# S4 convolution and gated feed-forward on one core: the first table's inputs go to the head of one queue, the spectrum products are merged, and the order ahead of the gate tiles is rewritten

## The chip, the cores and the metric

The kernel runs on one core of a Trainium2 chip. The metric is the device time of one execution in microseconds (us). Three runs of the kernel before took 786.79, 787.2 and 788.53 us; the median is 787.2. The profile comes from a further execution that took 788.84 us, of which the trace shows a span of 787.0 us from the first to the last instruction.

## The reference

The block takes a sequence of 2048 tokens of 448 channels through a state-space convolution and a gated feed-forward network, both conditioned by one vector `c`.

```python
mod = (_silu(c) @ w_mod).reshape(c.shape[0], 6, 1, -1)     # sa, ca, ga, sb, cb, gb
h = _layernorm(x) * (1 + ca) + sa
x = x + ga * S4(h)
h = _layernorm(x) * (1 + cb) + sb
x = x + gb * ((_gelu(h @ w_gate) * (h @ w_up)) @ w_down)
# S4(h): dt = exp(log_dt);  P = exp(dt * A * l) for l = 0..2047   (complex)
#        K = real(sum over n of C * P * (dt * B));  y = irfft(rfft(h) * rfft(K)) + h * Dskip
```

There are 448 channels with 256 complex states each. The kernel `K` (448 x 2048) has to be generated from the parameters before it can be transformed.

## The kernel before, in words

Every piece of work is a task with a name, made by `add(name, {engine: ...}, ...)`. The table `PLACE` gives each task a number. `Plan.run` sorts all tasks by that number and lets each issue its instructions in that order, so the table alone decides what follows what on each engine's in-order queue. A letter behind a number chooses the engine where a task may run on several (`a` ScalarE, `d` VectorE, `s` SyncE's queue, `p` GpSimd's). In the trace ScalarE is ACT, VectorE DVE, TensorE PE, GpSimd POOL and SyncE SP.

The program has four stages.

1. **Preparation.** `prep(t)` turns the parameters of 112 channels into two tables of logarithms and phases (`p.A1` to `p.f1`), split into bf16 pieces, written to memory (`p.put0`, `p.put1`, tile `lh_d`) and read back in another layout (`lt0`, `lt1`, tile `lt`). It needs the six parameter planes `in_abc` (`p.ld`: four planes, then two) and the step `dt` (`c.ld`, `dt`). For the first table its steps on ACT are `p.S1` (squares, absolute values), `p.S2` (logarithm, line 569), `p.S3` (exponential, line 570), `p.S4` (arctangent, line 580). Functions of different kinds need ACT_TABLE_LOAD ahead of them. At the same time the modulation rows come from `w_mod` (`m.ld`, `m.mm`, `m.ev`), and the input is normalised (`bn`, `norm`).
2. **Table stage (the K stage below).** For each of 56 sub-blocks of 8 channels: PE multiplies the small tables (`x.mm`, `y.mm`, `ang`), ACT takes exponentials (tiles `mx` and `my`), sines and cosines (`fg`), DVE forms the products `tx` (line 721) and `ty` (line 725), and PE sums over the states (`kgen`, line 748; tile `kg`). Every two sub-blocks are evacuated (`kev`, tile `ke`), turned (`ka`) and stored (`kout`, tile `ako`). `NMY` is the number of `my` buffers. Beside that runs the transform of the input (`ub`, `ub.ev`, tile `uo`) and, from about 205 us, the transform of `K` for two groups of channels, in 11 batches each (`k_fft`): `f.fwd` (line 1094), the spectrum product `f.pr` (line 1098), `f.inv` (line 1105), `f.z` (tile `zo`), `f.st`.
3. **Transition.** The third group is transformed with all engines free (`t_fft`). Its results go through memory: `t.s0` stores to `yb_d` (line 1224), `yi.l0` and `yi.l1` read it back (line 1297, tile `yi`). Then the residual (`co.mml`, line 1409; `co.addl`), the second layer norm, and the first gate tile. The first weights `w` are loaded meanwhile (`w.le`, line 1332). `spin` tasks are matrix products whose result is not used.
4. **Gate tiles.** Gate and up products (`gu`, lines 1524 and 1530) and down products (line 1630), for four blocks of 512 tokens.

A DMA is given one of eight completion semaphores in turn, and an issue waits until the earlier transfer on its semaphore has landed; `waits DMAHW4` in the listings below is such a wait (or one for data). The queue of SP issues in order, so a transfer that waits holds all behind it.

Of the kernel before, what the change touches and what calls it, by code (L numbers as in the profile page):

```python
# [15 lines left out]
AF = mybir.ActivationFunctionType  # L16
# [24 lines left out]
    "anc": "125 131 142 164 160 200 209 244 266 311 327 339 347 355 438 456 470 487 499 524",  # L41
    "ang": "114 115 130 146 158 162 204 212 241 298 319 324 341 350 421 443 454 476 496 506 511 591 602 610 654 670 690 698 "
        "741 761 764 775 792 795 805 885 894 905 908 927 932 950 1007 1018 1021 1034 1039 1051 1115 1124 1135 1151 1157 "
        "1169 1187 1197",
    "as": "66d 64d 79d 107d 116d 151d 119d 185a 250d 258d 265a 289d 309d 333d 334d 365d",
    "bn": "47 50 54 49 9 20 10 17 227 243 235 239 187 224 197 210",
    "c.ai": "1257",
    "c.ak": "177",
    "c.au": "62",
    "c.c": "21",  # L50
    "c.ea": "59",
    "c.ih": "1283",
    "c.ld": "11",
    "c.rd": "58",
    "c.t1": "219",
    "co.adde": "1329 1347 1366 1355",
    "co.addl": "1384 1387 1421 1410",
    "co.addx": "1495 1510 1499 1522 1672 1712 1735 1684 1791 1803 1809 1801",
    "co.ca": "1404a 1408a 1456a 1441a",
    "co.cb": "1415d 1416a 1459a 1448a",  # L60
    "co.h0": "1398a 1403a 1447d 1430a",
    "co.h2": "1534a 1580a 1571a 1562a 1748a 1744d 1755a 1760d 1848d 1882a 1833a 1866a",
    "co.l0": "1402 1405 1449 1434",
    "co.l2": "1541 1585 1573 1577 1749 1751 1757 1761 1849 1885 1843 1876",
# [36 lines left out]
    "dn3h": "1997 1999",
    "dn4": "1746 1889 1987",
# [1731 lines left out]
```

## Time and profile before

| what | value |
|---|---|
| median of three runs | 787.2 us |
| profiled execution: its time, its span | 788.84 us, 787.0 us |
| PE busy | 728.1 us, 93% of the span |
| DVE busy | 591.6 us, 75% |
| ACT busy | 459.5 us, 58% |
| POOL busy | 9.0 us, 1% |
| mean granted TensorE clock | 0.991 |
| moved by DMA | 139.87 MB |

Shares over the whole span hide that the stages differ. Before 336 us, ACT and DVE are nearly always busy; after 393 us only PE is. The first table product on PE starts at 28.39 us, the first exponential on ACT at 29.74 us, the first gate tile at 392.57 us. The profile's parts are: busy time of the engines, the span in slices, DMA queues, the chain of work that ended last, the costliest groups of instructions, and DMA issues. The trace also answers with a timeline (start, duration, engine, line, operation, and in brackets what ended the idle time ahead of it) and with busy times in chosen stretches.

### The profile page before, as it was taken

Reading aid. Unit: us, or ns where it says so; the run is one execution under the profiler, and the core shown is the slowest. Engines: PE = TensorE matmul, PEld = TensorE weight load, DVE = VectorE, ACT = ScalarE, POOL = GpSimd, SP = SyncE. Lnnn points to the kernel's source line nnn. Section 1 sums busy time; section 2 is a strip of 40 time slices with the busy share of each in tenths; the row PEclk is TensorE's granted clock in tenths of the full one; section 3 lists DMA queues with packets and bytes.
Section 4 is the critical chain, followed back from the end, with each engine's and each line's share of the span. In section 5 each row is a group of like instructions: output and inputs, shape, how many; then the busy total and the mean of one; then the engine's idle time right before and its main releaser. Section 6 shows DMA issues by size and latency. Waiting matters only on the chain.

```text
span 787.0 us, 19037 instructions
## 1 busy us (share of the span) xinstructions
PE 728.1 (93%) x8166; PEld 443.6 (56%) x8166; DVE 591.6 (75%) x893; ACT 459.5 (58%) x611; POOL 9.0 (1%) x24
## 2 busy tenths in 40 slices
PE   1786889998899999989999999999999999999998
PEld 0333454543667767768784445444595446944478
DVE  5989999999999999988768851469773587133743
ACT  4799999899999999961555640233421244012320
POOL 0000000000000000000300000000000000000000
PEclk9989899999999999999999999999999999999999
DMA  9654458997878767999697875345447324012201
GB/s 260 180 162 141 142 148 242 298 263 225 255 232 223 222 190 212 290 294 252 193 311 231 273 191 159 129 129 188 164 67 206 111 94 134 14 47 94 82 2 59
DMA packets 103790, 139.87 MB, mean 178 GB/s; under 512 B 34388, under 2 KB 85268, under 8 KB 103706
## 3 DMA queue, kind: packets, MB, share of 16 engines
q1 hardware_dynamic: 99940, 131.61, 57.0%
q10 hardware_dynamic: 3206, 6.07, 2.3%
q8 instruction: 64, 1.05, 0.6%
q0 software_dynamic: 560, 0.98, 0.4%
q14 instruction: 20, 0.16, 0.1%
HBM read 100.39 MB, written 36.01 MB: 173 GB/s over the span
## 4 chain that ended last, share of the span: by engine, by line
PE 69%; DVE 4%; ACT 4%; DMA 2%; issue 2%; SPq 1%; DVEq 0%; ACTq 0%
PE pq L1530 31%; PE pq L1630 9%; PE pf L1105 4%; PE pd L1599 4%; PE kg L748 4%; PE pf L1094 3%; PE pg L675 2%; PE pq L1524 2%; PE kg L771 2%; PE pd L1630 2%; DVE ty L725 1%; PE pd L1404 1%; PE pg L657 1%; ACT fg L692 1%; PE pf L1189 1%
## 5 line engine op out<-in xcount | busy, mean ns | idle before, releaser
L1530 PE MATMUL pq<-ht,wr 128*128 128x512 f16 (+1 forms) x1200 | 248.5, 365 | 1.3 <-DMA ht<-hl 1.2
L1530 PEld LDWEIGHTS <-wr 128*128 128x128 f16 x1200 | 114.5, 98 | 130.0 <-issue 13.0
L725 DVE TENSOR_TENSOR ty<-my,fg 128x2048 f32<-128x2048 f32 x56 | 127.5, 2283 | 0.8 <-issue 0.5
L1537 ACT ACTIVATE ge<-pq 128x512 f32<-128x512 f32 (+1 forms) x60 | 33.9, 565 | 102.1 <-PE pq L1524 68.7
L1544 DVE TENSOR_TENSOR fq<-ge,pq 128x512 f32<-128x512 f32 (+1 forms) x60 | 38.9, 649 | 71.5 <-PE pq L1530 44.3
L1556 ACT ACTIVATE hh<-fq 128x1024 f16<-128x1024 f32 (+1 forms) x49 | 46.7, 961 | 64.9 <-DVE fq L1544 46.4
L721 DVE TENSOR_TENSOR tx<-mx,fg 128x1024 f32<-128x1024 f32 x56 | 67.7, 1218 | 2.4 <-ACT fg L692 1.0
L1630 PE MATMUL pq<-d,hh 128*128 128x224 f16 x476 | 68.9, 259 | 0.0
L748 PE MATMUL kg<-ty,tx 128*32 128x64 f32 x3584 | 63.6, 222 | 4.7 <-issue 2.6
L748 PEld LDWEIGHTS kg<-ty,tx 128*32 128x32 f32 x3584 | 53.8, 111 | 23.8 <-issue 15.7
L1559 DVE TENSOR_TENSOR hlo<-fq,hh 128x1024 f16<-128x1024 f32 (+1 forms) x49 | 53.7, 1106 | 12.9 <-ACT hh L1556 12.7
L1630 PE MATMUL pq<-d,hlo 128*128 128x224 f16 x238 | 61.6, 259 | 0.0
L688 ACT ACTIVATE fg<-pg 128x1024 f32<-128x1024 f32 x56 | 58.0, 1038 | 1.2 <-PE pg L675 0.8
L662 ACT ACTIVATE my<-pg 128x1024 f32<-128x1024 f32 x56 | 55.5, 1031 | 2.0 <-PE pg L657 1.9
L1630 PEld LDWEIGHTS <-hh 128*128 128x128 f16 x560 | 54.1, 98 | 0.9 <-issue 0.2
L1105 PE MATMUL pf<-q,fc 128*128 128x160 f32 x264 | 41.5, 307 | 1.1 <-DVE q L1098 1.1
L692 ACT ACTIVATE fg<-fg,small 128x1024 f32<-128x1024 f32 x36 | 41.5, 1170 | 0.1
L1747 ACT ACTIVATE d<-fq 128x896 f16<-128x896 f32 x14 | 13.3, 947 | 46.1 <-PE pd L1599 27.3
L1105 PEld LDWEIGHTS pf<-q,fc 128*128 128x128 f32 x264 | 36.4, 190 | 6.5 <-issue 1.5
L675 PEld LDWEIGHTS <-lt 64*128 64x128 bf16 x304 | 18.0, 96 | 38.8 <-issue 26.5
L675 PE MATMUL pg<-ea,lt 64*128 64x512 bf16 x152 | 30.5, 392 | 7.6 <-ACT fg L699 3.4
L984 PE MATMUL pf<-ui,fu 128*128 128x448 f32 x66 | 31.0, 575 | 1.6 <-ACT uo L480 1.4
(210 smaller groups left out, 1117.6 us busy)
## 6 DMA issues: line engine op xcount, KB each, us to landing
wr<-w_d SPq DMA_DIRECT2D x21, 896.0 KB, 5.2
fc<-in_k_fc SPq DMA_DIRECT2D x20, 576.0 KB, 3.7
u_d<-so SPq DMA_DIRECT2D x32, 224.0 KB, 2.8
ui<-u_d SPq DMA_DIRECT2D x10, 672.0 KB
fq<-in_wd SPq DMA_DIRECT2D x14, 448.0 KB, 6.1
w<-in_wgu SPq DMA_DIRECT2D x11, 512.0 KB, 7.4
us<-uo SPq DMA_DIRECT2D x22, 240.0 KB, 5.2
q<-us SPq DMA_DIRECT2D x22, 240.0 KB, 6.4
```

Source lines behind the costliest of these rows:

```text
L662: A.activation(yb.tile.rearrange("p h (n k) -> p n h k", n=2), pb.tile.rearrange("p (n h k) -> p n h k", n=2, h=2), AF.Exp)
L675: T.matmul(pa[:, nh * 512:nh * 512 + 512], w, x, start=(k == 0), stop=(k == 2))
L688: A.activation(fb.tile[:, 0].rearrange("p x (n k) -> p n x k", n=2), pb.tile.rearrange("p (n x k) -> p n x k", n=2, x=2), AF.Sin, scale=TW ...
L692: A.activation(fb.tile[:, 1], fb.tile[:, 1], AF.Sin, scale=-TWO_PI, bias=halfpi)
L721: V.tensor_mul(tx.tile, xb.tile[:, xm, None, :].to_broadcast([128, 2, 512]), fb.tile[:, :, 0])
L725: V.tensor_mul(ty.tile, yb.tile[:, :, None, :].to_broadcast([128, 2, 2, 512]), fb.tile[:, None, :, 1].to_broadcast([128, 2, 2, 512]))
L748: T.matmul(kg[32 * g:32 * g + 32, 2 * (s % 2) + q, :64], tx[:, r, nh, 4 * q + g], ty[:, 0:4:3, nh, 4 * q + g] if r else ty[:, 1:3, nh, 4 * ...
L1105: T.matmul(pz.tile[:, e % 32 - sl0], fc.tile[:, i, 1 + t], pp.tile[:, t, i], start=(t == 0 and e != 32), stop=(t == 1 and e != 0))
L1530: T.matmul(pb.tile[k][:, ts], wr.tile[:, 4 * lo + t, k, c0:c0 + 128], ht[:, m, ts], start=f % 2 == 0 and i == 0, stop=f % 2 == 1 and i == 9)
L1556: A.activation(hg.tile[0][:, cb, c], fq.tile[:, c], AF.Copy)
L1559: V.tensor_sub(hg.tile[1][:, cb, c], fq.tile[:, c], hg.tile[0][:, cb, c])
L1630: T.matmul(bank(k)[:, m], x[:, p, q[0], ts], w[:, p, q[1]], start=new and m == 0 and p == 0 and z == 0, skip_group_check=True, stop=i in ( ...
```

## The change

- The first table's two parameter loads move from ACT's queue to SP's: the first is SP's first transfer, ahead of `ld`, `c` and the tokens `xt`; the second follows `xt`. The write of constant ones to `lh_d` (`pad`) moves from POOL's queue to SP's.
- In `prep`, the logarithm is kept in another slot, so that the exponential of it no longer has to precede the scaled copy. For the first table two one-element activations load the table of the logarithm (`pre.ln`) and of the arctangent (`pre.at`) ahead of their use.
- The spectrum product of a batch is one DVE instruction over 2 x 480 elements, in which the second factor is read twice, in place of two over 480 elements.
- `NMY` is 12 in place of 9. The room comes from POOL's descriptor space in SBUF, 2048 bytes per partition in place of the default.
- `PLACE` has new numbers for everything ahead of the gate tiles; behind them the numbers move by 2 and the order stays. Evacuations are dealt out anew: ACT has 19 of the 28 `ke` copies in place of 11, 15 of the 16 `uo` copies in place of 11, 17 `so` in place of 19, 9 `zo` copies of 480 columns in place of 13, 6 of the casts of `lh` in place of 8; DVE has the rest. The number of ACT_TABLE_LOADs is 43 in both kernels, the number of matrix products is the same.

```diff
 PLACE = {
-    "c.ld": "11",
+    "c.ld": "3",
...
-    NMY, NMX = 9, 5
+    NMY, NMX = 12, 5
...
+    PRE_LN = add("pre.ln", {"ACT": 0.2}, -8.4, lambda: A.activation(dump, eps, AF.Ln), [t_dt], table=LN)
...
-            (dma if t else adma)(b3.tile[:, :2] if i else b1.tile, a["abc"][t, :, 4:] if i else a["abc"][t, :, :4])
+            dma(b3.tile[:, :2] if i else b1.tile, a["abc"][t, :, 4:] if i else a["abc"][t, :, :4])
...
-        PAD[t] = add("pad", {"SP": 0.7} if t else {"POOL": 1.0}, v0 + 0.5, lambda: (dma if t else P.dma_start)(lh_d[t, :, :, 6:], a["k_one"][t]), [L0], kb=300)
+        PAD[t] = add("pad", {"SP": 0.7}, v0 + 0.5, lambda: dma(lh_d[t, :, :, 6:], a["k_one"][t]), [L0], kb=300)
...
-        S2 = op("S2", {"ACT": 0.28}, lambda: A.activation(x(10), x(3), AF.Ln), [B1, L3], LN, k=0.6)
-        S3 = op("S3", {"ACT": 0.28}, lambda: A.activation(x(2), x(10), AF.Exp, scale=0.5), [S2], EXP, k=0.65)
+        S2 = op("S2", {"ACT": 0.28}, lambda: A.activation(x(7), x(3), AF.Ln), [B1, PRE_LN if t == 0 else None], LN, k=0.6)
+        S3 = op("S3", {"ACT": 0.28}, lambda: A.activation(x(2), x(7), AF.Exp, scale=0.5), [S2], EXP, k=0.65)
...
+        pre_at = add("pre.at", {"ACT": 0.2}, v0, lambda: A.activation(dump, eps, AF.Arctan), [S3], table=ATAN) if t == 0 else None
...
-        B2 = op("B2", {"ACT": 0.28}, lambda: A.activation(x(10), x(10), AF.Identity, scale=0.5, bias=ld[:, t:t + 1]), [S2, S3], k=0.7)
+        B2 = op("B2", {"ACT": 0.28}, lambda: A.activation(x(10), x(7), AF.Identity, scale=0.5, bias=ld[:, t:t + 1]), [S2, L3], k=0.7)
...
         def prod():
-            for t in range(2):
-                V.tensor_mul(pp.tile[:, t, :ne], ut.tile[:, t, :ne], pk.tile[:, :ne])
+            V.tensor_mul(pp.tile[:, :, :ne], ut.tile[:, :, :ne], pk.tile[:, None, :ne].to_broadcast([128, 2, ne, n]))
...
-    nc = _bacc.Bacc("TRN2", target_bir_lowering=False, num_devices=1)
+    nc = _bacc.Bacc("TRN2", target_bir_lowering=False, num_devices=1, dynamic_dma_scratch_size=2048)
```

The lines of the changed program stand 2 to 5 numbers later than those of the program before (569 is 573, 1098 is 1102, 1332 is 1336).

**SP's queue at the start.** `in_abc` are the parameters, `in_A_u` the tokens, `in_w_mod` the modulation weights, `lh_d` the table written by line 595. Before:

```order
L852 DMA xt<-in_A_u 128x1792
L486 DMA ld<-in_A_log_dt 112x4
L486 DMA c_sb<-in_c 112x4
L805 DMA fg<-in_w_mod 112x1792 x3
L852 DMA xt<-in_A_u 128x1792
L595 DMA lh_d<-lh 112x1536
L486 DMA rd<-in_k_rd 128x1025
L486 DMA ea<-in_k_ea 128x1536
L486 DMA au<-in_k_au 128x128
L620 DMA lt<-lh_d 64x7x128 x2
```

Now:

```order
L515 DMA q<-in_abc 112x1024
L488 DMA ld<-in_A_log_dt 112x4
L488 DMA c_sb<-in_c 112x4
L857 DMA xt<-in_A_u 128x1792
L515 DMA q<-in_abc 112x512
L810 DMA fg<-in_w_mod 112x1792 x2
L857 DMA xt<-in_A_u 128x1792
L810 DMA fg<-in_w_mod 112x1792
L518 DMA lh_d<-in_k_one 224x512
L600 DMA lh_d<-lh 112x1536
```

The parameters and the ones stand in this queue now; `rd`, `au`, `ea` and the two `lt` loads follow as before.

**ACT in the preparation.** Line 551 is `p.S1`, 569 `p.S2`, 570 `p.S3`, 561 and 577 the copies `p.A3` and `p.B2`, 564 and 565 `p.C1`, 792 the sigmoid of `c`. Before:

```order
L564 ACTIVATE q<-q,dts__106 112x256
L565 ACTIVATE q<-q 112x256
L551 ACTIVATE q<-q 112x512
L552 ACTIVATE q<-q 112x256
L569 ACT_TABLE_LOAD
L569 ACTIVATE q<-q 112x256
L792 ACT_TABLE_LOAD
L792 ACTIVATE sig<-c_sb 112x4
L561 ACTIVATE q<-q,dts__106 112x256
L570 ACTIVATE q<-q 112x256
L577 ACTIVATE q<-q,ld 112x256
```

Now:

```order
L555 ACTIVATE q<-q 112x512
L556 ACTIVATE q<-q 112x256
L500 ACT_TABLE_LOAD
L500 ACTIVATE small<-small 128x1
L573 ACTIVATE q<-q 112x256
L568 ACTIVATE q<-q,dts__106 112x256
L569 ACTIVATE q<-q 112x256
L582 ACTIVATE q<-q,ld 112x256
L565 ACTIVATE q<-q,dts__106 112x256
L574 ACT_TABLE_LOAD
L574 ACTIVATE q<-q 112x256
L580 ACT_TABLE_LOAD
```

The load for the logarithm no longer waits for line 558 of DVE; the four copies stand between the logarithm and the exponential now.

**SP's queue at the end of the transition,** from the last store of the third group's results to the last of their read-backs. Before:

```order
L1224 DMA yb_d<-z_5275 128x128 [waits DMAHW3_49,Activation_49]
L1332 DMA w<-in_wgu 128x1024 [waits DMAHW4_49,DVE_49,PE_49]
L1297 DMA yi<-yb_d 8x2x512 [waits DMAHW7_49,DMAHW5_49]
L1297 DMA yi<-yb_d 6x2x512 [waits DMAHW6_49]
L1297 DMA yi<-yb_d 8x2x512
L1297 DMA yi<-yb_d 6x2x512 [waits DMAHW2_49]
L1297 DMA yi<-yb_d 8x2x512 [waits DMAHW3_49]
L1297 DMA yi<-yb_d 8x2x512 [waits DMAHW4_49]
```

Now:

```order
L1336 DMA w<-in_wgu 128x1024 [waits DMAHW3_49,DVE_49,PE_49]
L1301 DMA yi<-yb_d 8x2x512 [waits DMAHW4_49]
L1301 DMA yi<-yb_d 6x2x512 [waits DMAHW5_49]
L1228 DMA yb_d<-z_5248 128x128 [waits DMAHW7_49,DVE_49]
L1301 DMA yi<-yb_d 8x2x512 [waits DMAHW1_49,DMAHW0_49]
L1301 DMA yi<-yb_d 6x2x512 [waits DMAHW2_49]
L1301 DMA yi<-yb_d 8x2x512 [waits DMAHW3_49]
L1301 DMA yi<-yb_d 8x2x512 [waits DMAHW4_49]
L1301 DMA yi<-yb_d 8x2x512 [waits DMAHW7_49,DMAHW5_49]
```

The weight load stands ahead of the last store now. It is also the transfer whose semaphore a read-back near the end takes over.

More of the change, by code (lines that the diff above doesn't have):

```diff
@@ L510, in ld1 @@
                 b1.tile = pq.tile([DT, 4, N], FT, name="q")
-            (dma if t else adma)(b3.tile[:, :2] if i else b1.tile, a["abc"][t, :, 4:] if i else a["abc"][t, :, :4])
-        L0 = add("p.ld", {"SP" if t else "ACT": 0.42 if t else 0.1}, v0, lambda: ld1(0), (), [b1], (), kb=459)
-        PAD[t] = add("pad", {"SP": 0.7} if t else {"POOL": 1.0}, v0 + 0.5, lambda: (dma if t else P.dma_start)(lh_d[t, :, :, 6:], a["k_one"][t]), [L0], kb=300)
+            dma(b3.tile[:, :2] if i else b1.tile, a["abc"][t, :, 4:] if i else a["abc"][t, :, :4])
+        L0 = add("p.ld", {"SP": 0.42}, v0, lambda: ld1(0), (), [b1], (), kb=459)
+        PAD[t] = add("pad", {"SP": 0.7}, v0 + 0.5, lambda: dma(lh_d[t, :, :, 6:], a["k_one"][t]), [L0], kb=300)
         L3 = add("p.al", {"NONE": 0.0}, v0, al3, (), [b3])
-        L1 = add("p.ld", {"SP" if t else "ACT": 0.42 if t else 0.1}, v0, lambda: ld1(1), [L0, L3], (), [b3], kb=230)
+        L1 = add("p.ld", {"SP": 0.42}, v0, lambda: ld1(1), [L0, L3], (), [b3], kb=230)
         def op(n, e, fn, deps, table=None, alloc=(), use=(), k=0.0):
@@ L575, in slope @@
             V.tensor_mul(x(5), x(5), x(1))
+        pre_at = add("pre.at", {"ACT": 0.2}, v0, lambda: A.activation(dump, eps, AF.Arctan), [S3], table=ATAN) if t == 0 else None
         D1 = op("D1", {"DVE": 2.41}, slope, [S3], k=0.75)
-        B2 = op("B2", {"ACT": 0.28}, lambda: A.activation(x(10), x(10), AF.Identity, scale=0.5, bias=ld[:, t:t + 1]), [S2, S3], k=0.7)
+        B2 = op("B2", {"ACT": 0.28}, lambda: A.activation(x(10), x(7), AF.Identity, scale=0.5, bias=ld[:, t:t + 1]), [S2, L3], k=0.7)
         B3 = op("B3", {"DVE": 0.33}, lambda: V.tensor_add(x(10), x(10), x(4)), [B2], k=0.8)
         P0 = pieces(0, l0, lambda: pair(b3, 1), [A3, B3], 0.9)
-        S4 = op("S4", {"ACT": 0.28}, lambda: A.activation(x(5), x(5), AF.Arctan), [D1], ATAN, k=1.0)
+        S4 = op("S4", {"ACT": 0.28}, lambda: A.activation(x(5), x(5), AF.Arctan), [D1, pre_at], ATAN, k=1.0)
         G1 = op("G1", {"DVE": 0.33}, lambda: V.scalar_tensor_tensor(x(11), x(6), 126.0 / math.pi, x(0), op0=OP.mult, op1=OP.add), [C2, B1], k=0.9)
@@ L586, in phase @@
             V.scalar_tensor_tensor(x(7), x(11), -0.25 * math.pi, x(7), op0=OP.mult, op1=OP.add)
-        E1 = op("E1", {"DVE": 0.66}, phase, [S4, G1], k=1.1)
+        E1 = op("E1", {"DVE": 0.66}, phase, [S4, G1, B2], k=1.1)
         E2 = op("E2", {"ACT": 0.28}, lambda: A.activation(x(11), x(7), AF.Copy, bias=MAGIC), [E1], k=1.2)
```

440 rows, old and new, of the table PLACE are left out of this document.

## The prediction

> **What bounds the kernel now.** I read the busy times by stage first, because shares of the whole span mix stages with different limits. The columns are the stretch, its length, the busy time of PE, its weight loads, DVE, ACT and POOL with counts, then the TensorE clock, the DMA share and GB/s.
>
> ```profile
> 0.00:29.00 29.00, 11.70 (x31) 4.78 (x32) 18.77 (x46) 14.76 (x25) 1.51 (x11) 1.00 0.82 232
> 29.00:205.00 176.00, 147.23 (x2417) 74.41 (x2417) 167.88 (x232) 168.19 (x217) 0.00 (x0) 0.96 0.71 206
> 205.00:336.00 131.00, 128.51 (x2466) 95.77 (x2459) 126.03 (x129) 125.98 (x147) 0.00 (x0) 1.00 0.77 230
> 336.00:393.00 57.00, 51.35 (x806) 43.04 (x798) 47.70 (x79) 25.37 (x48) 6.83 (x12) 1.00 0.84 241
> 393.00:787.00 394.00, 389.31 (x2480) 225.60 (x2477) 231.24 (x411) 125.18 (x179) 0.69 (x1) 1.00 0.45 135
> ```
>
> The reader is to see four limits. Up to 29 us no engine is busy: a chain of steps and transfers sets the time. From 29 to 336 us DVE (293.9 of 307) and ACT (294.2) are both at 96%, and from 205 us PE is at 98%. From 336 to 393 us a chain runs over several engines. After 393 us PE is at 99%, and as the change leaves the order there as it was, I cost those 394 us at nothing: PE itself is the cover. A gain can come from the first 393 us only, and whatever starts the gate tiles earlier moves the end by as much.
>
> Next the timeline of the preparation (start, duration, engine, line, shapes, idle time ahead and its cause).
>
> ```profile
> 7.87 1.23 DVE L542 TENSOR_TENSOR q<-q 112x1024 f32<-112x1024 f32 x1 [6.96 <-DMA q<-in_abc]
> ...
> 12.54 1.28 ACT L569 ACT_TABLE_LOAD   x1 [0.76 <-DVE q L558]
> ...
> 13.83 0.42 ACT L569 ACTIVATE q<-q 112x256 f32<-112x256 f32 x1
> ...
> 14.27 1.28 ACT L792 ACT_TABLE_LOAD   x1
> ...
> 16.07 0.40 ACT L570 ACTIVATE q<-q 112x256 f32<-112x256 f32 x1
> ...
> 17.39 0.42 DVE L573 SCALAR_TENSOR_TENSOR q<-q 112x256 f32<-112x256 f32 x1
> ...
> 21.15 0.69 DVE L538 TENSOR_TENSOR lh<-q,lh 112x512 bf16<-112x512 f32 x1
> ...
> 21.92 0.31 SPq L595 DMA_DIRECT2D lh_d<-lh  x1
> ...
> 24.95 1.35 SPq L620 DMA_DIRECT2D lt<-lh_d  x2
> ...
> 28.40 0.28 PE L638 MATMUL pg<-rd,lt 64*128 64x256 bf16 x1 [0.69 <-DMA lt<-lh_d]
> ...
> 27.91 0.53 ACT L833 ACTIVATE gs<-pf 128x448 f32<-128x448 f32 x1
> 29.74 1.02 ACT L644 ACTIVATE mx<-pg 128x1024 f32<-128x1024 f32 x1
> ```
>
> The chain is: parameters land at 7.87, logarithm 13.83, exponential 16.07, the first pieces are split by 21.84, their store is issued at 21.92, the read-back at 24.95 (it waits for the store, 3.03), the first product at 28.40, the first exponential of the table stage at 29.74.
>
> **Part 1, the start.** The parameters shared the engines with the tokens. Now their 448 KB go first. The rows of 2 us give the rates:
>
> ```profile
> 0.00:20.00 20.00, 3.56 (x11) 1.30 (x12) 10.18 (x27) 9.75 (x16) 1.51 (x11) 1.00 0.91 258
> ...
> 0.00:2.00 2.00, 0.00 (x0) 0.00 (x0) 0.09 (x2) 0.32 (x1) 1.24 (x11) 1.00 0.36 47
> ...
> 4.00:6.00 2.00, 0.00 (x0) 0.00 (x0) 0.00 (x0) 0.00 (x0) 0.00 (x0) 1.00 1.02 317
> ...
> 12.00:14.00 2.00, 0.00 (x0) 0.00 (x0) 1.93 (x7) 1.45 (x2) 0.00 (x0) 1.00 0.99 247
> ...
> 20.00:22.00 2.00, 2.00 (x4) 0.77 (x4) 1.93 (x5) 0.42 (x1) 0.00 (x0) 1.00 0.02 7
> ```
>
> Transfers begin near 1.7 us (47 GB/s in the first 2 us); 459 kB at 247 to 317 GB/s take 1.5 to 1.9 us, so with about half a us to report the first product of the preparation starts near 4.3, 3.6 earlier. The logarithm gains another 1.0, since its load no longer stands between DVE and it: -4.6. Then four copies (0.45 each, an estimate from the 0.40 of line 570) and a load stand ahead of the exponential: 0.42 + 1.8 + 1.28 = 3.5 in place of 2.24, so -3.3. DVE has nothing else to finish when the exponential ends (before, line 573 came 0.9 after it): -4.2, and the store is issued at 17.7.
>
> There it meets what the move put ahead of it. SP's queue holds 5.16 MB before the store: by the row of the first 20 us (258 GB/s x 20 us) that is all that moved until the DMA engines fell idle (0.02 in 20 to 22 us). Nothing was taken away, so the queue is empty at about 20.0 again, and the store lands 2.7 later (as 22.23 to 24.95), at 22.7: -2.3. If all went at 317 GB/s, the queue would be empty at 18.0, and the gain would be capped by the rows of modulation: their last weights are the next thing late, with line 833 behind them, at about -3.1. If SP's queue alone goes at 247, it is empty at 22.6 and the store lands at 25.3: +0.4. **Start: -2.3, between -3.1 and +0.4**, by the row over 20 us, which holds the same transfers.
>
> The 247 GB/s stand where SP's queue was alone, the 317 where ACT's and POOL's queues ran beside it. [...]
>
> The two one-element activations cost 0.2 each and are covered: the first while DVE works on the squares, the second while it works on the reciprocal; without that cover they would cost 0.4. [...] The trace has the next activation 0.01 behind the load (12.54 + 1.28 to 13.83), and so I take 1.28.
>
> **Part 2, the table stage.** Prices are from start to start, since neighbours overlap:
>
> ```profile
> 322.14 0.57 ACT L480 ACTIVATE zo<-pf 128x480 f32<-128x480 f32 x1
> ...
> 322.59 0.39 ACT L480 ACTIVATE ke<-kg 128x252 f32<-128x252 f32 x1
> ...
> 322.85 1.04 ACT L680 ACTIVATE fg<-pg 128x1024 f32<-128x1024 f32 x1
> ...
> 333.34 0.41 DVE L482 COPY ke<-kg 128x252 f32<-128x252 f32 x1
> ...
> 333.67 0.15 DVE L766 TENSOR_TENSOR ke<-kg,d 128x4 f32<-128x4 f32 x1
> ...
> 328.80 1.21 DVE L1098 TENSOR_TENSOR q<-q,pf 128x480 f32<-128x480 f32 x2
> ...
> 329.93 0.16 DVE L766 TENSOR_TENSOR ke<-kg,d 128x4 f32<-128x4 f32 x1
> ...
> 330.00 1.22 DVE L721 TENSOR_TENSOR tx<-mx,fg 128x1024 f32<-128x1024 f32 x1
> ...
> 331.13 2.29 DVE L725 TENSOR_TENSOR ty<-my,fg 128x2048 f32<-128x2048 f32 x1
> ...
> 338.50 0.38 ACT L480 ACTIVATE ke<-kg 128x252 f32<-128x252 f32 x1 [1.34 <-PE kg L748]
> ```
>
> A pair of products occupies DVE for 1.13 us, and so does one product of 1024 elements; one of 960 is 64 elements shorter, about 0.07. The merging gives 22 x 0.07 = 1.5 us, not the 22 x 0.14 that durations without overlap suggest (two of 0.65 against 1.22 - 0.07). Eight `ke` copies less are 8 x 0.33 = 2.6 us of DVE. The other copies that change sides (`uo`, `zo`, `so`, `lh`, one `mag`), by the same rows and their widths, give back 1.5. DVE: -2.6. ACT: eight `ke` at 0.26 and four `uo` at 0.43, against four `zo` of 480 at 0.45, two `so`, two casts and one `mag` of 0.90: +0.3. ACT and DVE are equally full, so neither number is the term by itself; half of their sum is -1.15. PE has the same work. I take **-1.0**. One end is -6, if half of the 13 us that DVE and ACT each idle in this stage went with the rewritten order; the other is +3.9, if the `ke` and `uo` copies (2.1 + 1.8) all fall on ACT while it is the bound. The three further `my` buffers let exponentials run further ahead; ACT waits for no `my` buffer that I found, so I cost them at nothing.
>
> **Part 3, the transition.** The chain of work that ended last, SP's queue and PE:
>
> ```profile
> 375.52 0.32 SPq L1224 DMA_DIRECT2D yb_d<-z  x1
> ...
> 375.95 0.37 SPq L1332 DMA_DIRECT2D w<-in_wgu  x1
> ...
> 375.95 6.04 DMA w<-in_wgu
> ...
> 382.00 2.65 DMA yi<-yb_d
> ...
> 380.79 1.46 PE L1035 MATMUL pq<-idenh 128*128 128x512 f16 x6
> ...
> 385.11 0.66 PE L1409 MATMUL pd<-yi,ai 128*64 128x128 f32 x8 [1.11 <-DMA yi<-yb_d]
> ```
>
> The last read-back waited 6.04 us for a weight load that it does not use: it took over that load's semaphore. The load was held behind the last store (375.52). Now it stands ahead of it and may go about 2 us earlier. PE gets there earlier as well: it idled 1.11, and the idle products of 1.46 that stood ahead now stand behind. **-1.5**, between -2.6 (both of those) and 0, if the load waits for its buffer anyway. Next late is the layer norm between line 1409 and the first gate tile at 392.57, unchanged. The table load for the square root leaves this stretch; ACT was idle around it, so it counts nothing. POOL's transfers gain no work.
>
> **Sum.** -2.3 - 1.0 - 1.5 = -4.8. Against the profiled execution's own 788.84 (span 787.0 and 1.84 around it) that is 784.0; that execution was 1.64 above the median, so against the median 787.2 it is 782.4.
>
> **Rivals.** *More slack goes* (the end of part 2): -6 in place of -1.0 gives 777.4. For it speaks that three engines at 96 to 98% leave gaps that only an order decides; against it that the work of each is nearly unchanged. *The start gives nothing*: one queue at 247 GB/s, +0.4, and a transition at 0 with it, as its rows are about DMA too: 786.6. *ACT held by its copies*: each `ke` copy on ACT waits for PE's sums; the row at 338.50 lost 1.34 so. If the eight new ones all do, 8 x (1.34 + 0.26) = 12.8 replaces the -1.0: 796.2; it turns the change into a loss from three such waits on. Against it: most `ke` copies on ACT show no wait. *POOL starved by its smaller descriptor space*:
>
> ```profile
> yi<-yb_d POOLq DMA_DIRECT2D x9, 32.0 KB, 4.5
> ...
> 374.53 3.34 POOL L1297 DMA_DIRECT2D yi<-yb_d  x6
> ```
>
> Nine read-backs of 4.5 us, issued within 10 us now; one at a time they take 40, so +30, 812. Against it: they are small.
>
> **How the numbers follow.** Changes under 0.2% (1.6 us) cannot be told from none here. The forecast has 0.5, with its own range 779 to 785.5; more slack 0.2; nothing at the start 0.16; held copies 0.1; POOL 0.04. Faster: 0.5 + 0.2 and a little of the third, 0.73. Same: the rest of the third, 0.13. Slower: 0.14. From the ends -3.1 - 6 - 2.6 = -11.7 (775.5) and, with the third rival and a single held copy, +0.8 (788.0), the range is 776 to 788.
>
> **What would show it.** The first line-546 product near 4.3 us; the store at line 600 issued near 17.7 and the read-back near 22.7; the first exponential at 27.0 to 27.5; the last products of the table stage some 3 us earlier; a read-back that waits less than 6 us for `w`, and the first gate tile near 388. I would be wrong if the store waits longer in the queue than 5 us, if ACT shows new waits for PE ahead of `ke`, or if the gain of the first 30 us is given back before 336 because PE, and not ACT, sets the pace there.

## The result, and the profile after

The changed kernel takes 783.74 us (median of seven runs, 780.68 to 787.76); the kernel before, on the same chip, 787.2. The ratio is 0.9945, with a 95% interval of 0.9922 to 0.9967: 4.3 us less, between 2.6 and 6.1. A second set of eleven runs of the same program gave 0.9953 (0.9932 to 0.9974). The forecast was 782.4, range 776 to 788. Three single executions that took over 1.5% longer than the fastest of their kernel (one of after_again, one of tokens_fill, and one of queue_undone with 1463 us) are left out of all ratios and means.

The profiled execution took 782.35 us with a span of 780.4. Its busy times by stage, with the last cut 2 us behind the first gate tile (386.86); columns as in the prediction (PE, weight loads, DVE, ACT, POOL, granted clock, DMA share, GB/s):

```profile
0.00:29.00 29.00, 12.77 (x38) 5.09 (x39) 21.17 (x51) 18.01 (x30) 0.87 (x10) 1.00 0.83 245
29.00:205.00 176.00, 146.99 (x2440) 75.86 (x2439) 170.58 (x223) 171.06 (x227) 0.00 (x0) 0.99 0.73 209
205.00:336.00 131.00, 126.79 (x2544) 95.73 (x2546) 124.46 (x111) 124.73 (x145) 0.00 (x0) 1.00 0.84 241
336.00:389.00 53.00, 49.08 (x686) 42.11 (x683) 44.98 (x82) 23.01 (x42) 7.56 (x13) 1.00 0.79 232
389.00:780.00 391.00, 387.46 (x2464) 224.25 (x2462) 229.17 (x405) 122.77 (x175) 0.00 (x0) 1.00 0.44 134
```

Between 29 and 205 us DVE and ACT each do some 2.8 us more than before, and in the granted clock 0.99 stands where 0.96 stood. From the first gate tile to the end of the span it is 393.5 us, before 394.4. There PE waited once, for a transfer, and after the change it waits for none:

```profile
464.18 0.38 PE L1530 MATMUL pq<-ht,wr 128*128 128x512 f16 x1 [1.23 <-DMA ht<-hl]
```

The table stage alone, from the first exponential to the end of the last `kgen` product, before and after:

```profile
29.74:352.24 322.50, 288.59 (x5232) 181.07 (x5234) 308.05 (x370) 304.03 (x375) 0.00 (x0) 0.98 0.74 219
27.18:345.80 318.62, 284.55 (x5232) 180.79 (x5234) 306.15 (x343) 303.66 (x380) 0.00 (x0) 0.99 0.78 226
```

It is 3.9 us shorter. DVE's work fell by 1.9 us and its idle time by 2.0 (14.45 to 12.47), ACT's work by 0.4 and its idle time by 3.5 (18.47 to 14.96). The start, from the timeline:

```profile
4.47 1.23 DVE L546 TENSOR_TENSOR q<-q 112x1024 f32<-112x1024 f32 x1 [3.56 <-DMA q<-in_abc]
...
8.58 0.63 DVE L882 BATCH_NORM_STATS2 st<-xt 128x6 f32<-128x448 f32 x1 [2.09 <-DMA xt<-in_A_u]
...
9.80 0.42 DVE L560 TENSOR_TENSOR q<-q 112x256 f32<-112x256 f32 x1
...
10.84 0.42 ACT L573 ACTIVATE q<-q 112x256 f32<-112x256 f32 x1 [1.87 <-DVE q L562]
...
14.21 0.42 ACT L574 ACTIVATE q<-q 112x256 f32<-112x256 f32 x1
...
18.93 0.34 SPq L600 DMA_DIRECT2D lh_d<-lh  x1
...
22.00 1.35 SPq L625 DMA_DIRECT2D lt<-lh_d  x2
...
25.30 0.28 PE L643 MATMUL pg<-rd,lt 64*128 64x256 bf16 x1
...
27.18 1.02 ACT L649 ACTIVATE mx<-pg 128x1024 f32<-128x1024 f32 x1
```

The first product starts 3.4 earlier, the logarithm (10.84) 3.0, the store 3.0, the read-back 2.95, the first exponential 2.56. The parts of the chain of work that ended last in the transition:

```profile
368.48 3.74 DMA w<-in_wgu
...
375.21 3.46 DMA idenh<-in_k_ih
378.78 0.66 PE pd L1413 x8
```

The instructions around them:

```profile
370.60 0.37 SPq L1228 DMA_DIRECT2D yb_d<-z  x1
...
375.01 0.54 POOL L1301 DMA_DIRECT2D yi<-yb_d  x1 [2.50 <-DMA yb_d<-z]
...
386.86 2.35 PE L1534 MATMUL pq<-ht,wr 128*128 128x256 f16 x20
```

The chain names the constant `idenh`, which this product does not read; POOL's last read-back, issued at 375.01 after it had waited 2.50 for the last store, would land at about 378.7 by the median of these transfers (3.7). From the last store to the residual product it is now 8.18 us (370.60 to 378.78), before 9.59. The wait for `w` is 3.74 in place of 6.04.

What the column of the clock hides in long stretches shows in rows of 2 us. Before:

```profile
34.00:36.00 2.00, 1.34 (x8) 0.58 (x9) 1.89 (x5) 1.91 (x4) 0.00 (x0) 1.00 0.72 169
36.00:38.00 2.00, 0.80 (x6) 0.52 (x7) 2.00 (x6) 2.00 (x5) 0.00 (x0) 0.67 0.92 272
38.00:40.00 2.00, 2.00 (x8) 0.56 (x8) 1.28 (x5) 1.83 (x3) 0.00 (x0) 0.50 0.37 133
40.00:42.00 2.00, 2.00 (x12) 0.99 (x10) 1.51 (x5) 1.68 (x2) 0.00 (x0) 0.50 0.00 0
42.00:44.00 2.00, 2.00 (x12) 0.75 (x9) 0.41 (x2) 1.94 (x2) 0.00 (x0) 0.62 0.00 0
44.00:46.00 2.00, 1.53 (x16) 0.62 (x12) 2.00 (x4) 1.74 (x2) 0.00 (x0) 1.00 0.25 56
```

After, the only such place of the whole trace:

```profile
70.00:72.00 2.00, 0.65 (x22) 0.28 (x11) 1.90 (x7) 2.00 (x4) 0.00 (x0) 1.00 0.00 2
72.00:74.00 2.00, 1.33 (x40) 0.91 (x43) 1.97 (x4) 2.00 (x4) 0.00 (x0) 0.89 0.03 8
74.00:76.00 2.00, 2.00 (x46) 1.20 (x38) 2.00 (x4) 1.97 (x3) 0.00 (x0) 0.50 0.00 0
76.00:78.00 2.00, 2.00 (x12) 0.77 (x9) 1.77 (x6) 1.53 (x3) 0.00 (x0) 0.76 0.00 0
```

PE runs at half its clock for 6.8 us before (the missing shares 0.33 + 0.50 + 0.50 + 0.38 of 2 us are 3.4 us of clock, twice that in time), and once more so from 77.7 to 84.5; after, for 3.4 us. Each follows a stretch in which PE had little to do (0.65 of 2 us after; before, 0.52 at 74 to 76 us for the second). What the other engines do meanwhile differs. The two stretches before and the one after:

```profile
36.70:43.50 6.80, 5.95 (x24) 2.52 (x24) 4.09 (x12) 6.25 (x9) 0.00 (x0) 0.50 0.28 99
77.70:84.50 6.80, 6.21 (x80) 3.04 (x76) 6.76 (x14) 6.11 (x9) 0.00 (x0) 0.50 0.05 17
73.60:77.00 3.40, 3.40 (x66) 1.89 (x57) 3.36 (x9) 2.91 (x5) 0.00 (x0) 0.50 0.02 5
```

In the first, DVE is idle for 2.7 us, waiting for PE's products (0.41 of 2 us busy at 42 to 44 us). In the other two DVE stays busy and ACT is idle for 0.7 and 0.5 us.

### The profile page after: what moved, and what is told of

The parts are those of the page before. It is cut to its first block, busy times and chain, and to the rows that moved or that the text cites. A ratio compares the mean times of both kernels' runs of the same rounds, so it can differ in the third digit from the quotient of the medians.

```text
span 780.4 us, 18984 instructions
## 1 busy us (share of the span) xinstructions
PE 723.1 (93%) x8166; PEld 443.0 (57%) x8166; DVE 590.4 (76%) x868; ACT 459.6 (59%) x616; POOL 8.4 (1%) x23
## 4 chain that ended last, share of the span: by engine, by line
PE 69%; ACT 12%; DMA 4%; DVE 3%; issue 2%; SPq 1%; DVEq 0%; ACTq 0%
PE pq L1534 31%; PE pq L1634 9%; PE pd L1603 4%; PE kg L753 4%; PE pf L1109 4%; PE pg L680 3%; ACT my L667 2%; PE pq L1528 2%; PE pf L1099 2%; ACT fg L693 2%; PE kg L776 2%; PE pd L1634 2%; DMA us<-uo 2%; ACT fg L697 2%; PE pf L989 1%
## 5 line engine op out<-in xcount | busy, mean ns | idle before, releaser
L753 PE MATMUL kg<-ty,tx 128*32 128x64 f32 x3584 | 61.7, 222 | 2.2 <-issue 1.3
L1109 PE MATMUL pf<-q,fc 128*128 128x160 f32 x264 | 41.4, 307 | 0.3 <-issue 0.3
L697 ACT ACTIVATE fg<-fg,small 128x1024 f32<-128x1024 f32 x36 | 41.4, 1163 | 0.0
L776 PE MATMUL kg<-ak,ke 128*64 128x128 f32 x448 | 30.5, 279 | 3.4 <-DVE ke L771 3.4
```

Of the source, the lines that this page charges most:

```text
L697: A.activation(fb.tile[:, 1], fb.tile[:, 1], AF.Sin, scale=-TWO_PI, bias=halfpi)
L753: T.matmul(kg[32 * g:32 * g + 32, 2 * (s % 2) + q, :64], tx[:, r, nh, 4 * q + g], ty[:, 0:4:3, nh, 4 * q + g] if r else ty[:, 1:3, nh, 4 * ...
L1109: T.matmul(pz.tile[:, e % 32 - sl0], fc.tile[:, i, 1 + t], pp.tile[:, t, i], start=(t == 0 and e != 32), stop=(t == 1 and e != 0))
```

## The experiments

The ratio is to the runs of the kernel before on the same chip, with its 95% interval; the clock is the mean of the mean granted clocks of these runs. Behind it stands what one profiled execution of each shows, in us: first exponential, from there to the end of the last `kgen` product, clock lost to half clock between 29 and 336 us (the missing shares in rows of 2 us, added up), from the last `kgen` product to the first gate tile.

| kernel | ratio (95%) | clock | first exp. | table stage | clock lost | transition |
|---|---|---|---|---|---|---|
| before | 1 | 0.988 | 29.74 | 322.5 | 6.8 | 40.3 |
| after | 0.9945 (0.9922-0.9967) | 0.996 | 27.18 | 318.6 | 1.7 | 41.1 |
| after_again | 0.9953 (0.9932-0.9974) | 0.996 | 28.29 | 318.6 | 3.4 | 41.5 |
| start_alone | 0.9993 (0.9973-1.0013) | 0.988 | 28.28 | 322.9 | 10.3 | 42.2 |
| table_order_undone | 1.0003 (0.9974-1.0032) | 0.986 | 28.61 | 321.0 | 8.5 | 43.5 |
| trans_order_undone | 0.9960 (0.9942-0.9979) | 0.995 | 28.06 | 320.7 | 8.5 | 42.6 |
| two_products | 0.9941 (0.9915-0.9966) | 0.993 | 27.68 | 317.5 | 1.7 | 39.3 |
| queue_undone | 1.0031 (1.0005-1.0056) | 0.990 | 35.12 | 317.3 | 3.0 | 41.4 |
| no_preload | 0.9954 (0.9931-0.9977) | 0.995 | 30.12 | 318.4 | 5.1 | 41.3 |
| tokens_later | 0.9908 (0.9871-0.9945) | 0.997 | 28.24 | 316.0 | 1.7 | 38.8 |
| readback_pool | 0.9942 (0.9909-0.9975) | 0.995 | 27.47 | 322.8 | 5.1 | 41.9 |
| before_fill | 1.0024 (1.0002-1.0047) | 0.994 | 30.02 | 322.6 | 5.1 | 40.3 |
| tokens_fill | 0.9970 (0.9942-0.9998) | 0.995 | 28.92 | 323.8 | 1.7 | 40.8 |
| store_ahead | 1.0026 (1.0005-1.0046) | 0.988 | 32.01 | 323.3 | 9.7 | 41.8 |

Kernels whose instructions of the start stand in the same order differ by up to 1.4 us in the first exponential (27.18 to 28.61; the tokens that DVE waits for there are used first at 8.55 to 9.68), and executions of one program differ in the number of half-clock stretches. So one profile of each says little about differences of 1 us; the ratios decide.

**start_alone.** Against the changed kernel:

```diff
-order after throughout
+order after for the first 58 tasks (to `p.put0`, `c.rd`, `rstd`, `rcp`), then the order of before
-    NMY, NMX = 12, 5
+    NMY, NMX = 9, 5
-            V.tensor_mul(pp.tile[:, :, :ne], ut.tile[:, :, :ne], pk.tile[:, None, :ne].to_broadcast([128, 2, ne, n]))
+            for t in range(2):
+                V.tensor_mul(pp.tile[:, t, :ne], ut.tile[:, t, :ne], pk.tile[:, :ne])
-    nc = _bacc.Bacc(..., dynamic_dma_scratch_size=2048)
+    nc = _bacc.Bacc(...)
```

> The kernel before with the new start alone: the parameters and the ones in SP's queue, the two one-element activations, the logarithm in its own slot, and the new order up to the first store and the constant `rd` (58 tasks). Behind it the old order, the old products, nine `my` buffers. Theory A (the gain of the start reaches the end): first exponential at 27.2 us in place of 29.74, last `kgen` product and first gate tile some 2.5 earlier than before's 352.0 and 392.6, time 0.997 of before (784.7). Rival B (the table stage takes it back, since its pace is set by PE behind 205 us or by a wait for a transfer): first exponential at 27.2, but the first gate tile within 0.7 of 392.6 and the time within 0.1% of before.

The first exponential came at 28.28, 1.5 earlier, and the first gate tile at 393.32, not earlier than before's 392.57. The runs gained 0.6 us by the ratio, between a gain of 2.1 and a loss of 1.0. Its window from 29 to 205 us has a granted clock of 0.94:

```profile
29.00:205.00 176.00, 150.37 (x2425) 75.97 (x2423) 167.57 (x230) 167.82 (x217) 0.00 (x0) 0.94 0.71 204
```

The full -2.3 does not reach the end when the table stage is the old one; a part of it may. The rival holds by the time; theory A's 0.997 lies just outside the interval.

**table_order_undone.** The start, the merged products, the twelve buffers and the transition stay.

```diff
-order after throughout
+order after for the first 58 tasks, then the order of before up to its number 1240, then the order after
```

> The changed kernel with the old order of the table stage (the evacuations dealt out as before too); new start, merged products, twelve `my` buffers and the new order of the transition stay. Theory A (about 2 of the 3.9 us that the table stage lost between the two profiles are the clock's, 0.66 in two stretches of 10 us before; the rest is order and merged products in equal parts): 1 us slower than the changed kernel, ratio to before 0.9955. Rival B (the order is what gained): 3 to 4 us slower than the changed kernel, ratio 0.998 to 1.000. Rival C (the order gains nothing): same as the changed kernel, 0.9945.

1.0003: all of the gain is gone, and rival B holds. Everything else that the change does is in this kernel, so nothing of the gain is left without the new order of the table stage. Whether that order pays without the rest is open: no run has it with nine `my` buffers, and none puts it alone into the kernel before. The clock of this kernel is that of before, 0.95 from 29 to 205 us:

```profile
29.00:205.00 176.00, 149.10 (x2428) 76.34 (x2429) 168.39 (x230) 168.63 (x218) 0.00 (x0) 0.95 0.71 206
```

**trans_order_undone.**

```diff
-order after throughout
+order after for the first 1255 tasks, then the order of before
```

> The changed kernel with the old order from the last `kgen` product on (transition; behind it nothing differs). Theory A (the transition became 0.8 us longer, as the profiles show: 40.6 us from the last `kgen` product to the first gate tile before, 41.4 after): 0.8 us faster than the changed kernel, ratio to before 0.9935; a read-back waits some 6 us for `w` again. Rival B (the step of the prediction, -1.5 for the weight load that stands ahead, is right and the profile's +0.8 is chance): 1.5 us slower than the changed kernel, ratio 0.9965.

0.9960 against 0.9945 and 0.9953: some 1 us slower than the changed kernel, with an interval that takes in no difference. The sign is rival B's, so the step in the prediction is not refuted, and theory A's 0.9935 lies outside the interval. From the last store to the residual product it is 9.26 us here, as before (9.59) and unlike after (8.18):

```profile
373.60 0.32 SPq L1228 DMA_DIRECT2D yb_d<-z  x1
...
382.86 1.12 PE L1413 MATMUL pd<-yi,ai 128*64 128x128 f32 x8 [2.39 <-DMA yi<-yb_d]
```

**two_products.**

```diff
-            V.tensor_mul(pp.tile[:, :, :ne], ut.tile[:, :, :ne], pk.tile[:, None, :ne].to_broadcast([128, 2, ne, n]))
+            for t in range(2):
+                V.tensor_mul(pp.tile[:, t, :ne], ut.tile[:, t, :ne], pk.tile[:, :ne])
```

> The changed kernel with two spectrum products of 480 elements per batch in place of the one of 960, everything else as it is. Theory A (the prediction's price: 22 x 0.07 = 1.5 us of DVE, half of it on the path): 0.8 us slower than the changed kernel, ratio to before 0.9955. Rival B (PE sets the pace behind 205 us, so DVE's 1.5 us are hidden): no difference, 0.9945. Rival C (an instruction costs more than it occupies, 22 x 0.14): 3 us slower, 0.998.

0.9941: no difference from the changed kernel, as rival B has it. In the table stage DVE is busy for 1.2 us more (307.39 us against 306.15), 0.06 for each pair, so the price of 0.07 was about right and the time does not show it. That PE hides it fits (the products lie behind 205 us, where PE is at 97 to 98%) but was not tested by itself.

**queue_undone.**

```diff
-            dma(b3.tile[:, :2] if i else b1.tile, ...
+            (dma if t else adma)(b3.tile[:, :2] if i else b1.tile, ...
-            dma(lh_d[t, :, :, 6:], a["k_one"][t])
+            (dma if t else P.dma_start)(lh_d[t, :, :, 6:], a["k_one"][t])
```

> The changed kernel with the first table's two parameter loads back in ACT's queue and the write of ones back in POOL's; everything else, the order too, as it is. Theory A (the parameters land early because they go ahead of the tokens, not because of their queue; in ACT's queue they share the engines with them): first product of the preparation at 7 to 8 us in place of 4.47, first exponential 2 us later (29.2), the end 1.5 to 2 us later than the changed kernel, ratio to before 0.997. Rival B (the start's path is held by the tokens, which DVE waits for until 8.58 in the changed kernel, so that the parameters matter less): first exponential within 1 us of 27.2, end within 1 us of the changed kernel, 0.995.

Neither theory holds. The first product is nearly as early as in the changed kernel (4.85), but the whole is slower than before:

```profile
4.85 1.22 DVE L546 TENSOR_TENSOR q<-q 112x1024 f32<-112x1024 f32 x1 [3.94 <-DMA q<-in_abc]
...
16.76 0.51 ACT L568 ACTIVATE q<-q,dts__106 112x256 f32<-112x256 f32 x1 [5.50 <-DMA q<-in_abc]
...
24.55 0.32 SPq L600 DMA_DIRECT2D lh_d<-lh  x1
```

In the new order the second load stands behind ACT's squares, so ACT issues it at 6.91, and it lands behind what SP's queue has issued by then, at 16.7. That fits a load that waits for the bytes issued ahead of it, on whatever queue: the first load, in ACT's queue too, came within 0.4 us of its time in SP's. The run also prices a late start: the first exponential is 7 us later than in the other kernels with this table order (35.12 against some 28), and the time 790.7 is 6.8 above 783.9, of which the lower clock (0.990) may be half, by the slope given below.

**no_preload.**

```diff
-    PRE_LN = add("pre.ln", ...)
-        pre_at = add("pre.at", ...)
-        S2 = op(..., [B1, PRE_LN if t == 0 else None], LN, k=0.6)
+        S2 = op(..., [B1], LN, k=0.6)
-        S4 = op(..., [D1, pre_at], ATAN, k=1.0)
+        S4 = op(..., [D1], ATAN, k=1.0)
```

> The changed kernel without the two one-element activations that load the tables of the logarithm and of the arctangent ahead of use; the number of table loads stays, they fall on the first real use. Theory A (the logarithm's load comes behind DVE's line 562 again, 1.28 less the 0.2 of the dummy, and the chain to the first store has nothing else to cover it): store of the first pieces and first exponential 1.2 us later, the end about 1 us later, ratio to before 0.996. Rival B (ACT is idle 1.87 us ahead of the logarithm, and a load does not wait for the data of the instruction behind it): no difference.

The load does wait for DVE (4.76 us idle ahead of it), the logarithm starts at 13.78 and the first exponential at 30.12, 2.9 us later each than in the changed kernel's profile:

```profile
12.49 1.28 ACT L570 ACT_TABLE_LOAD   x1 [4.76 <-DVE q L559]
13.78 0.42 ACT L570 ACTIVATE q<-q 112x256 f32<-112x256 f32 x1
```

Only 1.3 us of that are the load's: in this execution DVE had the tokens at 10.24, not at 8.58, and reached line 559 that much later. The time, 0.9954, is 0 to 1 us above the changed kernel and fits theory A, but its interval takes in no difference. The next activation stands 0.01 behind the load again (12.49 + 1.28 to 13.78), and in the kernel before a load starts at 14.27, 0.02 behind the end of the activation before it (13.83 + 0.42). So these rows price a load at its own 1.28 us.

**tokens_later.** The order of the tasks on DVE:

```diff
 p.A1 p.A2
-bn (first) sil2
 p.B1
+bn (first) sil2
 bn (second)
```

> The changed kernel with one thing moved on DVE: the statistics of the first tokens and the sigmoid's three steps stand behind the steps of lines 560 to 563, not ahead of them. In the changed kernel DVE waits 2.09 us for the tokens there (until 8.58) and reaches line 560 at 9.80. Theory A (that wait is what the prediction missed in the start: the logarithm came at 10.84 and not at 9.2): line 560 near 7.0, the logarithm at 9.0, the store of the first pieces 1.5 to 2 us earlier than 18.93, first exponential 1.5 earlier (25.7), end 1 to 1.5 us earlier than the changed kernel, ratio to before 0.993. Rival B (SP's queue is not empty before about 20 us, as the prediction had it): the store is issued earlier but lands when it did, first exponential within 0.4 of 27.2, no difference in time. Rival C (the modulation rows are late next, since their sigmoid comes later): first exponential later than 27.2.

```profile
9.13 0.40 ACT L573 ACTIVATE q<-q 112x256 f32<-112x256 f32 x1
...
17.80 0.33 SPq L600 DMA_DIRECT2D lh_d<-lh  x1
...
23.20 1.35 SPq L625 DMA_DIRECT2D lt<-lh_d  x2
...
28.24 1.02 ACT L649 ACTIVATE mx<-pg 128x1024 f32<-128x1024 f32 x1
```

The logarithm starts at 9.13, as the prediction had it, and the store is issued 1.1 earlier, but the read-back comes 5.4 us behind it, 1.2 later than in the changed kernel. So for the start rival B is right that an earlier store does not help; its "no difference in time" is not met. The kernel is the fastest, 781.61 us (six runs), ratio 0.9908, below both kernels by value, although its interval overlaps that of the changed kernel. As the first exponential is no earlier, its gain is not the one expected. Its clock is the highest (0.997 against 0.996), which by the slope given below is 0.5 us of some 2.6; the rest is open.

**readback_pool.**

```diff
-    yi.l0 of part 1 and yi.l1 of part 0 on SP
+    yi.l0 of part 1 and yi.l1 of part 0 on POOL
```

> The changed kernel with two of the read-backs of the third group issued by POOL in place of SP, so that SP issues the last store right behind the weight load and not 1.6 us later. In the changed kernel that store is issued at 370.60 while its data were ready at 369.06, and POOL's last read-back at 375.01 waits 2.50 for it. Theory A (this wait is what the transition lost): last store issued near 369.1, last read-back at 373.7, residual product (line 1413) 1.3 us earlier than 378.78, end 1.3 us earlier than the changed kernel, ratio to before 0.993. Rival B (seven issues of 0.7 on SP and their semaphores set the pace, or a semaphore of a weight load is taken over again): residual product within 0.4 of 378.8, no difference.

0.9942: no difference, rival B. SP issues the last store right behind the weight load now (0.5 us), but a read-back took over the semaphore of that load again, and the chain of work that ended last has

```profile
373.48 5.88 DMA w<-in_wgu
```

**before_fill.** In the kernel before (the same for line 657):

```diff
-                for m, s in enumerate(grp):
+                for m, s in [p for p in enumerate(grp) for _ in range(2 if sc < 3 else 1)]:
```

> The kernel before, with the products of lines 638 and 657 for the first three of eight sets of seven sub-blocks computed twice into the same place (the second result is the same), 168 products of 0.2 us in the first 100 us of the table stage, so that PE is idle less there. All orders are those of before. [...] Rival B (the clock does not follow PE's own idle time, or what it takes does not reach the end): clock 0.988, time as before or up to 2 us slower. Rival C (the added products delay ACT, which has nothing to spare): clock up, time up by 2 to 5 us.

The added products are 84, not 168 (the expectation counts their weight loads too), and by PE's busy time at their two lines they add 9.0 us (21.0 to 26.6 and 11.9 to 15.3 us), not 168 x 0.2 = 33.6. The clock rose from 0.988 to 0.994, which is about three half-clock stretches of 3.4 us per run in place of five or six; the time rose by 0.24% (0.02 to 0.47): rival C. So the clock does in part follow what PE does in these stretches. What the added products cost is told by the next run.

**tokens_fill.** The same products in the kernel of tokens_later.

> The changed kernel with the tokens' statistics moved behind lines 560 to 563 as in the run that moved them alone, and with the same products computed twice. Theory A (the clock): clock at 0.997 or more, 1 to 2 us faster than the changed kernel, ratio to before 0.992. Rival B (there are only one or two half-clock stretches left to remove, and the added products cost as much): same as the changed kernel, 0.9945. Rival C (they delay ACT): 2 to 5 us slower than the changed kernel.

0.9970: 4.5 us above tokens_later in the means of the runs (785.9 and 781.4), at nearly the same clock. So these products cost some 4 us where no half-clock stretch is to be removed, and 1.6 us where the clock rises by 0.006; the difference of 2 to 3 us is an estimate of what the clock gave back there, with a standard error of about 1.3.

**after_again.** No edit.

> The changed kernel once more, beside the two others, for more runs of it with their clocks. Theory A (the new order of the table stage sets the clock, not the chance of a run): mean clock of its runs between 0.993 and 0.998 and each above nearly all of before's (0.981 to 0.991); time 783 to 784.5, ratio 0.994 to 0.996. Rival B (the clock is chance of the chip and the hour): clock as that of the runs of before beside it, ratio 0.998 to 1.000.

Theory A: clock 0.996 in the mean (0.991 to 0.998), time 784.

**store_ahead.** SP's queue, on top of tokens_later:

```diff
-x.ld (second tokens)
 m.ld pad p.put0
+x.ld (second tokens)
 c.rd c.au
-c.ea
 lt0
+c.ea
```

> The changed kernel with the tokens' statistics moved behind lines 560 to 563 as before, and two transfers moved back in SP's queue: the second block of tokens behind the store of the first pieces, and the constant `ea` behind the read-back. Where only the statistics were moved, the store was issued at 17.80 in place of 18.93, but the read-back came at 23.20 in place of 22.00: the store waited in the queue. Theory A (the bytes ahead of the store in the queue hold it, as the prediction had it: 0.9 MB less there are 3.5 us at 258 GB/s): read-back issued at 20 to 21, first exponential at 26.0 to 27.0 in place of 28.24, end 1 us earlier than with the statistics moved alone (781.6), ratio to before 0.990. Rival B (the rows of modulation and the tokens' square root, which stand ahead of the first exponential on ACT, are as late, since the second tokens now land later): read-back early, first exponential at 27.8 or later, time as with the statistics moved alone, 0.991. Rival C (the order of transfers at the start also moves the half-clock stretches): clock below 0.993 and time 784 or more.

```profile
21.16 1.54 SPq L625 DMA_DIRECT2D lt<-lh_d  x2
...
26.12 0.63 DVE L882 BATCH_NORM_STATS2 st<-xt 128x6 f32<-128x448 f32 x1 [5.67 <-DMA xt<-in_A_u]
...
29.18 0.30 ACT L891 ACTIVATE rs<-mv,small 128x8 f32<-128x8 f32 x1 [4.67 <-DVE mv L883]
...
32.01 1.02 ACT L649 ACTIVATE mx<-pg 128x1024 f32<-128x1024 f32 x1
```

The read-back is 2.0 earlier than in tokens_later, so bytes ahead of the store do hold it. But DVE waits 5.67 us for the tokens and ACT 4.67 for DVE, and the first exponential is 3.8 later: rival B. The clock fell to 0.988 and the time is 1.0026: rival C as well. In the trace PE runs at half clock from 28 to 45 us without a break.

## Why the prediction was right, and where it was wrong

**The total.** -4.8 was forecast, -4.3 measured (2.6 to 6.1), and the direction was right. That the sum came so near is partly luck, since its terms missed in both directions. In the two profiles the start is 2.6 us shorter (2.3 forecast), the table stage 3.9 (1.0 forecast), the transition 0.7 longer (1.5 shorter forecast), and the gate tiles 0.9 shorter (nothing forecast). Together that is 6.6 in this pair of executions, of which the one before lay above its median and the one after below.

**The start, -2.3.** Its place was right, its reach was not. In the trace the first exponential is 2.56 earlier in one execution and 1.45 in another, against 2.2 to 2.7 forecast (27.0 to 27.5). The first product came at 4.47 (4.3 forecast; the terms given for it add up to 3.7 to 4.1, and no row shows the half a us to report among them; after, 540 kB had moved by 4.0 us, 0.47 ahead of that product), the store at 18.93 (17.7), the read-back at 22.00 (22.7). The step that failed inside is "the logarithm gains another 1.0": DVE stood 2.09 us waiting for the tokens, with five instructions ahead of line 560, so the logarithm came at 10.84 and not near 9.2. Moving them (tokens_later) brought 9.13, and the read-back came no earlier (23.20 against 22.00); store_ahead, with fewer bytes ahead of the store, had it at 21.16, which bears out the prediction's reason, the queue of SP. The first 20 us moved at 261 GB/s against 258 before:

```profile
0.00:20.00 20.00, 6.15 (x16) 2.43 (x16) 12.59 (x31) 10.62 (x20) 0.87 (x10) 1.00 0.88 261
```

so one queue lost nothing to three; the -3.1 that the prediction has for 317 GB/s did not come, since the rate stayed at 261, and the store itself was issued only at 18.93. (The 317 of 4 to 6 us had ACT's queue, 0.23 MB, beside SP's, 0.40 MB; POOL's moved nothing there.) The sentence "whatever starts the gate tiles earlier moves the end by as much" is right, but an earlier start does not start them as much earlier: alone it gave 0.6 us (a gain of 2.1 to a loss of 1.0), and in its profile the first exponential was 1.5 earlier and the first gate tile 0.8 later.

**The table stage, -1.0.** This is the term that was mis-sized. With the old order in its place 0.9945 and 0.9953 become 1.0003, so the order is worth some 4 us, and the merged products, which had 0.07 x 22 of DVE in the sum, nothing that can be measured. The step that failed is to let half of the summed busy times of ACT and DVE stand for the whole stage. As busy times they came out about right: -1.9 and -0.4, half of which is -1.1. What the sum left out is idle time, 2.0 us less on DVE and 3.5 less on ACT. The clock was at hand for it: in the row from 29 to 205 us the prediction showed a granted clock of 0.96 and did not use it. That is 6.8 us of missing clock in 176, 13.6 us at half speed. The runs show what goes with it. In 109 runs of the kernel before, the clock lies between 0.980 and 0.993 and the time falls by 5.9 us (standard error 0.6) for each 0.01 of it. From 0.988 to 0.996 that gives 4.8 us, as much as the whole measured gain. At a clock of 0.991 the kernel before takes 786.7 us (14 runs), and the kernels with the new table order and a first exponential by 30.2 us (after, after_again, trans_order_undone, two_products, no_preload, tokens_later, readback_pool) 786.7 (6 runs): at an equal clock no difference is left. One line of that slope through each of the two sets, 109 and 72 runs, puts them 0.2 us apart, with a standard error of 0.5.

That the order moves the clock is shown: the four kernels with the old order in the table stage have 0.986 to 0.988 (0.994 with the added products), the seven just named 0.993 to 0.997. It does not set it alone: with the new order and a late first exponential, queue_undone (35.12) and store_ahead (32.01) have 0.990 and 0.988, and no gain. That the clock is what makes the time is not shown to the same degree. Runs of one kernel go together with it, and before_fill and tokens_fill point the same way, but no experiment changed the clock and nothing else. In the profile before, DVE lost 2.7 us in one of the two stretches and nothing in the other, and the one after cost it nothing. Something in the timing that leaves PE idle could cause both the clock and the time. The rival *more slack goes* had the place and, at -6, was nearer than -1.0; and gaps of ACT and DVE, which it named as the reason, did go (3.5 and 2.0 us in the profiles). That PE's clock stood behind some of them it did not say.

**The transition, -1.5.** From the last store to the residual product the trace shows 8.18 in place of 9.59, which is the step as told. From the last `kgen` product to the last store it became 1.5 longer in the same execution (345.8 to 370.6, before 352.2 to 375.5), and the stage as a whole 0.7 longer (1.1 in after_again). The net of the order is open: the order undone costs some 1 us, with no difference inside the interval.

**The gate tiles, 0.** The prediction put them at nothing, with PE itself as the cover. PE was not cover throughout: its wait of 1.23 us for `ht` (above) is gone. All kernels with the twelve buffers and the smaller descriptor space take 393.1 to 393.5 us there, whatever their order; the three without (before, before_fill, start_alone) take 394.3 to 394.6, each with one wait of PE of 0.9 to 1.2 us for a transfer. Which of the two does it was not tried.

**The twelve buffers.** The prediction costs them at nothing as well. No run takes them away alone, so what they add to the new order is not known.

**The rivals.** *The start gives nothing* was near for what the start gave at the end and far for the rest. *ACT held by its copies* did not come: the waits of ACT for `kg` ahead of `ke` sum to 1.3 us in four waits, against 2.6 in two before. *POOL starved* did not come either: its read-backs landed in 3.7 us in place of 4.5.

## What to carry to other kernels

Read the granted clock in rows of 2 us before adding up busy times: a mean of 0.96 over 176 us was 13.6 us at half speed, and a sum that ignores it may leave out its largest term. Where an order written out by hand is changed, test the order apart from the code: here the merged products and the earlier loads, which the change names first, gave little that can be measured, and without the rearranged table stage nothing of the gain was left. Busy times alone do not make up a stage: look at the idle time as well, and at what ended it. The shorter start gave 0.6 us alone (at most 2.1); one that was 7 us longer cost 6.8, its lower clock included.

## What the runs showed of the hardware

The half-clock stretches come in steps. After, 3.4 us; before, 6.8 and 6.8 us; in the mean clock of the runs of all kernels the commonest values are 0.998, 0.996, 0.993, 0.991, 0.989 and 0.987, about 0.0022 apart, which is one stretch of 3.4 us at half speed in 787 us. One such step goes with 1.3 us of time (0.0022 x 5.9 per 0.01). In the 3.5 us ahead of the stretch after, PE was busy 1.48 us (42%), and in those ahead of the first one before 1.49 us, with no gap above 1.11 us:

```profile
70.00:73.50 3.50, 1.48 (x42) 0.70 (x34) 3.39 (x8) 3.50 (x5) 0.00 (x0) 1.00 0.00 1
```

```profile
33.00:36.50 3.50, 1.49 (x12) 0.69 (x12) 3.39 (x7) 3.41 (x7) 0.00 (x0) 1.00 0.54 123
```

The first row is of after, the second of before. So PE was at work for 42 to 43% of the time ahead of these two. A low share does not always cost the clock: in the kernel before PE was busy 1.15 of 3.4 us from 194.5 us on, and in the changed kernel still less,

```profile
31.00:34.40 3.40, 0.68 (x9) 0.21 (x6) 3.37 (x8) 3.21 (x6) 0.00 (x0) 1.00 0.70 162
34.40:37.80 3.40, 2.31 (x16) 0.90 (x16) 3.26 (x8) 2.61 (x5) 0.00 (x0) 1.00 0.88 241
```

and the clock stayed at 1.00 behind both. What tells the one case from the other was not shown. By its mean clock in a run, the changed kernel has one to four such stretches (0.998 to 0.991), the kernel before mostly four to seven (0.991 to 0.985 in 101 of 109 runs); what makes the number differ from run to run was not shown either.
